# One product of the rational unit moved from VectorE to GpSimd in sixteen units, with its constant added by ScalarE

## The chip, the core and the metric

The kernel runs on one core of a Trainium2 chip. The metric is the device time of one execution in microseconds (us), the median of several. Engines are TensorE (PE in the rows; PEld is its weight load), VectorE (DVE), ScalarE (ACT), GpSimd (POOL) and SyncE (SP), which issues DMAs.

## What is computed

Three stages follow each other: a gated linear attention (4 batches, 8 heads, 768 steps, head width 48), a two-layer network with a rational activation (384 to 2048 to 384, 3072 tokens), and a second network with a softmax-like activation and a layer norm (384 to 1024 to 384). The change touches the rational activation:

```python
h = x @ w_in
h2 = h * h
h3 = h2 * h
P = a[0] + a[1] * h + a[2] * h2 + a[3] * h3
Q = 1.0 + np.abs(b[0]) * np.abs(h) + np.abs(b[1]) * h2
g = P / (Q + 1e-06)
return (g @ w_out).astype(np.float32)
```

## The kernel before

The tokens are cut into 6 chunks of 512. For every chunk the hidden layer of 2048 is cut into 16 blocks of 128. One chunk with one block is a **unit**; there are 96, numbered u = 0 to 95, and the first 16 are the first chunk.

A unit has two halves. `m_up(u)` multiplies the block of `w_in` with the chunk (nine matmuls at L590: three slices of 128, each as high x high, high x low and low x high part), which leaves `hp`, 128 x 512, in PSUM; then it works out g in `p`; at the end ScalarE writes its high part `gh` (L623) and GpSimd the rest `gl` (L624). `m_down(u)` adds the unit's part to the three sums `x2p` (nine matmuls at L636) and is written four units later (LAG = 4).

With numerator and denominator brought to squares by constants, `p` starts as (h + beta1)^2 (L597) and `w` as (|h| + beta2)^2 (L598); Q up to a factor is then `w` plus a constant column, `rest`. ScalarE works out a first inverse as exp(-ln(w + rest)), and one Newton step makes it exact enough: inverse times (2 - Q times inverse). The product of Q and the first inverse is what the change is about. Two forms stand side by side:

- **even units below 24** (MIX): VectorE folds the numerator into `hp` (L608), ScalarE takes the logarithm (L609) and the exponential (L610) into `ah`, GpSimd adds `rest` to `w` (tensor_scalar, L611) and multiplies by `ah` (tensor_tensor, L612), VectorE multiplies numerator and inverse (L613) and finishes with L614. That makes three VectorE steps.
- **all others**: VectorE's L616, ScalarE's logarithm (L617) and exponential into `hp` (L618), then VectorE's L619 (the product, with the constant added), L620 and L621. That makes four VectorE steps.

Buffers: `hp` has three in PSUM, so unit u+3's first product waits for the last reader of unit u's. `ah`, `w`, `gh` and `gl` have two each, `p` three.

Beside the first 16 units two other strands run. Weights arrive in four groups of four blocks; `split_w` joins two words of a float64 into a float32 on VectorE (L535, L538, L539), takes the high part on ScalarE (L545) and the low part on GpSimd (L546). Groups 2 and 3 are split while units 0 to 8 run. And the attention of the following halves is prepared: transposes (L290, L295, L324) and scans (L308, L317) on VectorE, scores (L420), masks on GpSimd (L428), outputs (L444) and states (L483) on TensorE.

The order on each engine is not that of the source: a scheduler places every instruction from its own estimate of time, within dependences and buffers. Each engine then works through its order without overtaking.

Of the kernel before, what the change touches and what calls it, by code (L numbers as in the profile page):

```python
# [12 lines left out]
AF = mybir.ActivationFunctionType  # L13
ALU = mybir.AluOpType
# [16 lines left out]
def kernel(  # L31
# [15 lines left out]
    nc = tc.nc  # L47
# [9 lines left out]
    NF1 = DF1 // 128  # L57
# [21 lines left out]
    MIX = lambda u: u < 24 and u % 2 == 0  # L79
# [73 lines left out]
    def network(fast):  # L153
# [424 lines left out]
        fin = {}  # L578
# [4 lines left out]
        def m_up(u):  # L583
            c, f = divmod(u, NF1)
            n, o = divmod(f, 4)
            hp = ps_hp.tile([128, NTOK], F32, name="hp", tag="h")
            hi, lo = wi[n]
            for kt in range(KT):
                for w, xx in ((hi, 0), (hi, 1), (lo, 0)):
                    last["PE", u] = nc.tensor.matmul(  # L590
                        hp, lhsT=w[:, kt, 128 * o:128 * o + 128], rhs=xts[c][:, kt, xx, :],
                        start=(kt == 0 and w is hi and xx == 0), stop=(kt == KT - 1 and w is lo),
                    )
            ah, w, p = (moe_pool.tile([128, NTOK], F32, name=nm, tag=nm, bufs=NB[nm]) for nm in ("ah", "w", "p"))
            nc.scalar.activation(ah, hp, AF.Abs)  # L595
            if fast:
                nc.scalar.activation(p, hp, AF.Square, bias=co[:, 7:8])  # L597
                nc.scalar.activation(w, ah, AF.Square, bias=co[:, 6:7])  # L598
                rest = co[:, 8:9]
            else:  # L600
                nc.scalar.activation(p, hp, AF.Identity, bias=ab[:, 2:3], scale=ab[:, 3:4])
                nc.gpsimd.tensor_scalar(w, ah, babs[:, 1:2], babs[:, 0:1], ALU.mult, ALU.add)
                nc.gpsimd.tensor_tensor(w, w, ah, ALU.mult)
                nc.vector.tensor_tensor(p, p, hp, ALU.mult)
                rest = qc
            a1, a0 = (co[:, 9:10], a0s) if fast else (ab[:, 1:2], ab[:, 0:1])
            if fast and MIX(u):
                nc.vector.scalar_tensor_tensor(hp, p, a1, hp, ALU.add, ALU.mult)  # L608
                nc.scalar.activation(ah, w, AF.Ln, bias=rest)  # L609
                nc.scalar.activation(ah, ah, AF.Exp, scale=-1.0)  # L610
                nc.gpsimd.tensor_scalar(w, w, rest, 1.0, ALU.add, ALU.mult)  # L611
                nc.gpsimd.tensor_tensor(w, w, ah, ALU.mult)  # L612
                nc.vector.scalar_tensor_tensor(hp, hp, a0, ah, ALU.add, ALU.mult)  # L613
                fin[u] = nc.vector.scalar_tensor_tensor(p, w, 2.0, hp, ALU.subtract, ALU.mult, reverse0=True)  # L614
            else:
                nc.vector.scalar_tensor_tensor(p, p, a1, hp, ALU.add, ALU.mult)  # L616
                nc.scalar.activation(ah, w, AF.Ln, bias=rest)  # L617
                nc.scalar.activation(hp, ah, AF.Exp, scale=-1.0)  # L618
                nc.vector.scalar_tensor_tensor(w, w, rest, hp, ALU.add, ALU.mult)  # L619
                nc.vector.scalar_tensor_tensor(hp, w, 2.0, hp, ALU.subtract, ALU.mult, reverse0=True)  # L620
                fin[u] = nc.vector.scalar_tensor_tensor(p, p, a0, hp, ALU.add, ALU.mult)  # L621
            gh, gl = (moe_pool.tile([128, NTOK], F32R, name=nm, tag=nm, bufs=NB[nm]) for nm in ("gh", "gl"))
            last["ACT", u] = nc.scalar.activation(gh, p, AF.Copy)  # L623
            last["POOL", u] = nc.gpsimd.tensor_tensor(gl, p, gh[:].bitcast(F32), ALU.subtract)  # L624
            gts[u] = (gh, gl)
# [246 lines left out]
        for u in range(NU + LAG):  # L872
# [6 lines left out]
            if u < NU:  # L879
                if f == 0 and c == NCH - 1:  # L880
                    if fast:
                        judge(moe_pool)
                    open2()
                    tail = chain(w2_load("i"), n_load(0), w2_load("o"))
                if f == 0 and c and not fast:
                    x_load(c)
                if fast and u < NF1:
                    if f % 4 == 0:
                        _run(prep)
                        prep = w1_group(f // 4 + 2) if f < 8 else iter(())  # L890
                    with later(G1):
                        take(prep, 1)
                m_up(u)
                if fast and u < NF1:
                    with later(G1):
                        take(prep, 1)
# [157 lines left out]
```

## Time and profile before

| what | value |
|---|---|
| times of three runs | 785.37, 786.02, 788.82 us |
| median | 786.02 us |
| the profiled execution | 786.76 us |
| its span, first to last instruction | 784.9 us |
| mean granted TensorE clock | 0.962 |
| TensorE, busy | 730.2 us (93%) |
| VectorE, busy | 639.8 us (82%) |
| ScalarE, busy | 534.5 us (68%) |
| GpSimd, busy | 359.9 us (46%) |

A busy share over the whole span mixes stretches with different limits, so such a table only says where to look; what a step is worth is read in the stretch in which it runs. The granted clock is the share of TensorE's full speed (2.4 GHz) that the chip allowed.

### The profile page before, as it was taken

The page shows a single profiled execution, that of the slowest core. Times are in us where ns is not written, and L with a number is a line of the kernel's source. Part 1 is how long each engine was busy: PE and PEld are TensorE (multiplying, and loading weights), DVE is VectorE, ACT ScalarE, POOL GpSimd, SP SyncE. Part 2 cuts the span into 40 slices and gives each one's busy share as a digit, 9 for nine tenths or more (in the row PEclk, how much of TensorE's full clock was granted, in tenths as well). Part 3 has the DMA queues.
Part 4 walks back from the last instruction along what each step waited for, and adds up shares of the span by engine and source line. Part 5 has one row for each costly group of instructions (what it writes and reads, how often), then busy time and mean ns, then how long its engine had stood idle before and what let it go on. Part 6 is the DMA issues. An engine that isn't in the chain of part 4 may idle for free.

```text
span 784.9 us, 13904 instructions
## 1 busy us (share of the span) xinstructions
PE 730.2 (93%) x4976; PEld 605.3 (77%) x4976; DVE 639.8 (82%) x1110; ACT 534.5 (68%) x983; POOL 359.9 (46%) x306
## 2 busy tenths in 40 slices
PE   4775896999999999999999999999999999999996
PEld 3654674778887788777878788888888989988996
DVE  5999999989899998989898966567887688777640
ACT  2245656779886888788978888788865555555541
POOL 3256677766755344444554433243233433352322
PEclk9767699899999999999999999999999999999998
DMA  7865547373858175536736250640024353542552
GB/s 172 239 201 174 142 154 158 114 182 115 189 167 208 57 196 134 146 83 208 157 121 122 82 121 2 228 175 0 1 82 101 115 120 90 140 102 57 139 121 72
DMA packets 87278, 101.74 MB, mean 130 GB/s; under 512 B 34464, under 2 KB 63136, under 8 KB 87200
## 3 DMA queue, kind: packets, MB, share of 16 engines
q1 hardware_dynamic: 87104, 100.67, 48.5%
q8 instruction: 41, 0.67, 0.4%
q14 instruction: 37, 0.30, 0.1%
q10 hardware_dynamic: 96, 0.10, 0.0%
HBM read 60.59 MB, written 27.56 MB: 112 GB/s over the span
## 4 chain that ended last, share of the span: by engine, by line
DVE 28%; PE 17%; ACT 13%; issue 5%; SPq 4%; DMA 4%; POOL 1%; ACTq 0%; DVEq 0%; POOLq 0%
PE x2p L636 6%; PE hp L590 6%; DVE room L750 3%; SPq L760 3%; DVE room L733 2%; PE op L774 2%; ACT jk L735 2%; DVE p L616 2%; DVE hp L620 2%; DVE w L619 2%; DVE sm L729 2%; DMA room<-room 2%; DMA rq<-in_q_dram 2%; DVE room L748 2%; PE h L710 2%
## 5 line engine op out<-in xcount | busy, mean ns | idle before, releaser
L590 PE MATMUL hp<-xt,g 128*128 128x512 f32 x864 | 225.0, 402 | 9.5 <-DVE alT L302 4.0
L624 POOL TENSOR_TENSOR gl<-p,gh 128x512 fp32r<-128x512 f32 x96 | 127.9, 1332 | 190.2 <-ACT gh L623 104.1
L590 PEld LDWEIGHTS hp<-xt,g 128*128 128x128 f32 x864 | 163.2, 192 | 50.0 <-DVE p L621 5.0
L636 PE MATMUL x2p<-gh,g 128*128 128x512 f32 x576 | 197.5, 397 | 2.8 <-ACT x2e L644 2.1
L636 PEld LDWEIGHTS x2p<-gh,g 128*128 128x128 f32 x576 | 108.6, 189 | 30.5 <-ACT x2e L644 4.7
L636 PE MATMUL x2p<-gl,g 128*128 128x512 f32 x288 | 113.6, 394 | 1.8 <-POOL gl L624 1.8
L774 PE MATMUL op<-w2oh,room 128*128 128x384 f32 x384 | 101.8, 339 | 1.2 <-DVE room L766 0.6
L766 POOL TENSOR_TENSOR room<-room,room 128x1024 fp32r<-128x1024 f32 x22 | 54.6, 2484 | 101.1 <-ACT room L765 79.7
L619 DVE SCALAR_TENSOR_TENSOR w<-w,co,hp 128x512 f32<-128x512 f32 x84 | 62.0, 738 | 44.2 <-ACT hp L618 43.3
L710 PE MATMUL h<-w2ih,x 128*128 128x512 f32 x288 | 90.7, 394 | 0.0
L597 ACT ACTIVATE p<-hp,co 128x512 f32<-128x512 f32 x96 | 65.9, 687 | 13.0 <-POOL gl L624 12.8
L618 ACT ACTIVATE hp<-ah 128x512 f32<-128x512 f32 x84 | 50.1, 596 | 32.8 <-DVE p L616 31.6
L774 PEld LDWEIGHTS op<-w2oh,room 128*128 128x128 f32 x384 | 70.1, 188 | 2.8 <-DVE room L766 1.0
L616 DVE SCALAR_TENSOR_TENSOR p<-p,co,hp 128x512 f32<-128x512 f32 x84 | 61.8, 736 | 10.2 <-ACT p L597 9.9
L598 ACT ACTIVATE w<-ah,co 128x512 f32<-128x512 f32 x96 | 69.4, 724 | 0.7 <-DVE hp L620 0.3
L595 ACT ACTIVATE ah<-hp 128x512 f32<-128x512 f32 x96 | 56.5, 589 | 13.7 <-PE hp L590 13.6
L636 PEld LDWEIGHTS x2p<-gl,g 128*128 128x128 f32 x288 | 54.2, 188 | 15.0 <-POOL gl L624 3.1
L623 ACT ACTIVATE gh<-p 128x512 fp32r<-128x512 f32 x96 | 59.9, 624 | 7.8 <-PE x2p L636 2.7
L774 PE MATMUL op<-w2ol,room 128*128 128x384 f32 x192 | 65.0, 339 | 0.0
L710 PEld LDWEIGHTS h<-w2ih,x 128*128 128x128 f32 x288 | 53.9, 188 | 11.7
L621 DVE SCALAR_TENSOR_TENSOR p<-p,co,hp 128x512 f32<-128x512 f32 x84 | 61.9, 737 | 1.1
L617 ACT ACTIVATE ah<-w,co 128x512 f32<-128x512 f32 x84 | 60.5, 721 | 1.2
(168 smaller groups left out, 1274.8 us busy)
## 6 DMA issues: line engine op xcount, KB each, us to landing
room<-room SPq DMA_DIRECT2D x96, 128.0 KB, 2.4
qk_d<-qk SPq DMA_DIRECT2D x10, 771.0 KB, 4.4
st<-in_moe_w_in_dram SPq DMA_DIRECT2D x15, 512.0 KB, 4.6
st<-in_moe_w_out_dram SPq DMA_DIRECT2D x18, 384.0 KB, 3.5
qks<-qk_d SPq DMA_DIRECT2D x20, 257.0 KB, 5.2
x<-x_d SPq DMA_DIRECT2D x18, 256.0 KB, 3.4
out_dram<-o SPq DMA_DIRECT2D x94, 48.0 KB, 1.6
ra<-in_alpha_dram SPq DMA_DIRECT2D x44, 96.0 KB, 2.3
```

The lines of the kernel that those rows point to most:

```text
L590: last["PE", u] = nc.tensor.matmul(hp, lhsT=w[:, kt, 128 * o:128 * o + 128], rhs=xts[c][:, kt, xx, :], start=(kt == 0 and w is hi and xx = ...
L597: nc.scalar.activation(p, hp, AF.Square, bias=co[:, 7:8])
L598: nc.scalar.activation(w, ah, AF.Square, bias=co[:, 6:7])
L616: nc.vector.scalar_tensor_tensor(p, p, a1, hp, ALU.add, ALU.mult)
L617: nc.scalar.activation(ah, w, AF.Ln, bias=rest)
L619: nc.vector.scalar_tensor_tensor(w, w, rest, hp, ALU.add, ALU.mult)
L621: fin[u] = nc.vector.scalar_tensor_tensor(p, p, a0, hp, ALU.add, ALU.mult)
L623: last["ACT", u] = nc.scalar.activation(gh, p, AF.Copy)
L624: last["POOL", u] = nc.gpsimd.tensor_tensor(gl, p, gh[:].bitcast(F32), ALU.subtract)
L636: nc.tensor.matmul(x2ps[c][d], lhsT=w[:, o, 128 * d:128 * d + 128], rhs=gg, start=(f == 0 and w is hi and gg is gh), stop=(f == NF1 - 1 an ...
L710: nc.tensor.matmul(hp[:, 512 * n:512 * n + 512], lhsT=x2s[c][:, kt, x, CH * b:CH * b + CH], rhs=w2[w][:, kt, 512 * n:512 * n + 512], start ...
L774: nc.tensor.matmul(op, lhsT=x[:, 128 * f:128 * f + 128], rhs=w2[w][:, f, :], start=(f == 0 and x is hi and w == "oh"), stop=(f == NF2 - 1 ...
```

## The change

For u below NF1 = 16 every unit, odd or even, takes three VectorE steps and GpSimd's product. The constant that GpSimd added in the even units is now added by ScalarE, as an Identity activation with `rest` as its bias, between the logarithm and the exponential. Units 16 to 23 keep the form of before by parity, and the others their own.

```diff
             a1, a0 = (co[:, 9:10], a0s) if fast else (ab[:, 1:2], ab[:, 0:1])
-            if fast and MIX(u):
+            if fast and u < NF1:
+                nc.vector.scalar_tensor_tensor(hp, p, a1, hp, ALU.add, ALU.mult)
+                nc.scalar.activation(ah, w, AF.Ln, bias=rest)
+                nc.scalar.activation(w, w, AF.Identity, bias=rest)
+                nc.scalar.activation(ah, ah, AF.Exp, scale=-1.0)
+                nc.gpsimd.tensor_tensor(w, w, ah, ALU.mult)
+                nc.vector.scalar_tensor_tensor(hp, hp, a0, ah, ALU.add, ALU.mult)
+                fin[u] = nc.vector.scalar_tensor_tensor(p, w, 2.0, hp, ALU.subtract, ALU.mult, reverse0=True)
+            elif fast and MIX(u):
                 nc.vector.scalar_tensor_tensor(hp, p, a1, hp, ALU.add, ALU.mult)
                 nc.scalar.activation(ah, w, AF.Ln, bias=rest)
                 nc.scalar.activation(ah, ah, AF.Exp, scale=-1.0)
```

Since the scheduler lays out all engines anew, other work moves too. In the changed program the lines of the units below 16 are L608 (numerator), L609 (logarithm), L610 (constant), L611 (exponential), L612 (product), L613 and L614; `gh` is L631, `gl` L632, and L636 becomes L644.

VectorE, before, at the end of unit 9, whose tiles are `p_1335`, `w_1334` and `hp_1323` (`hp_1358` is unit 10, `hp_1424` unit 11, `ft_1241` the last weight split, `P_1413` a scan of the attention):

```order
L538 SCALAR_TENSOR_TENSOR ft_1241<-st_1242,ft_1241 128x384
L308 SCALAR_TENSOR_TENSOR P_1413<-alT_111,d1_109 128x774
L619 SCALAR_TENSOR_TENSOR w_1334<-w_1334,co_85,hp_1323 128x512
L539 SCALAR_TENSOR_TENSOR ft_1241<-st_1242,ft_1241 128x384
L608 SCALAR_TENSOR_TENSOR hp_1358<-p_1370,co_85,hp_1358 128x512
L620 SCALAR_TENSOR_TENSOR hp_1323<-w_1334,hp_1323 128x512
L616 SCALAR_TENSOR_TENSOR p_1436<-p_1436,co_85,hp_1424 128x512
L621 SCALAR_TENSOR_TENSOR p_1335<-p_1335,co_85,hp_1323 128x512
```

VectorE, changed, at the same place (unit 9 is `p_1339`, `hp_1327`; unit 10 `hp_1363`; the last weight split `ft_1244`):

```order
L302 MEMSET alT_111 128x6x2
L608 SCALAR_TENSOR_TENSOR hp_1327<-p_1339,co_85,hp_1327 128x512
L539 SCALAR_TENSOR_TENSOR ft_1244<-st_1245,ft_1244 128x384
L290 STREAM_TRANSPOSE alT_111<-ra_1152 128x2x4x32
L608 SCALAR_TENSOR_TENSOR hp_1363<-p_1375,co_85,hp_1363 128x512
L290 STREAM_TRANSPOSE alT_111<-ra_1152 128x2x4x32
L295 STREAM_TRANSPOSE alT_111<-ra_1152 128x4x32
L613 SCALAR_TENSOR_TENSOR hp_1327<-hp_1327,co_85,ah_1337 128x512
L295 STREAM_TRANSPOSE alT_111<-ra_1152 128x4x32
L308 SCALAR_TENSOR_TENSOR P_1418<-alT_111,d1_109 128x774
L614 SCALAR_TENSOR_TENSOR p_1339<-w_1338,hp_1327 128x512
```

Unit 9's last step now follows the scan at once, and the last weight split stands ahead of the transposes instead of behind the scan.

TensorE, before, around the first product of unit 11 (`hp_1424`; `sc` are scores, `gh_1271` and `gl_1272` belong to unit 7):

```order
L420 MATMUL sc_1385<-qks_112 128x128
L420 MATMUL sc_1386<-qks_112 128x128
L590 MATMUL hp_1424<-xt_356,g2_751 128x512 x9
L636 MATMUL x2p0_1091<-gh_1271,g1_629 128x512
L636 MATMUL x2p0_1091<-gl_1272,g1_629 128x512
```

TensorE, changed, at the same place (unit 11 is `hp_1429`; `gh_1197` and `gl_1198` belong to unit 6, `gh_1275` to unit 7):

```order
L420 MATMUL sc_1390<-qks_112 128x128
L420 MATMUL sc_1391<-qks_112 128x128
L644 MATMUL x2p0_1093<-gl_1198,g1_629 128x512
L644 MATMUL x2p0_1093<-gh_1197,g1_629 128x512
L644 MATMUL x2p1_1094<-gl_1198,g1_629 128x512
L644 MATMUL x2p1_1094<-gh_1197,g1_629 128x512
L644 MATMUL x2p2_1095<-gl_1198,g1_629 128x512
L644 MATMUL x2p2_1095<-gh_1197,g1_629 128x512
L644 MATMUL x2p0_1093<-gh_1275,g1_629 128x512
L644 MATMUL x2p1_1094<-gh_1275,g1_629 128x512
L644 MATMUL x2p2_1095<-gh_1275,g1_629 128x512
L590 MATMUL hp_1429<-xt_356,g2_751 128x512 x9
```

Nine matmuls of the second product, which all stood elsewhere, now stand between the scores and unit 11.

## Rows read from the trace of the kernel before

**Rows 1.** By stretch (us): length, PE, PEld, DVE, ACT, POOL busy, clock, DMA:

```profile
71.00:147.20 76.20, 58.29 (x370) 44.30 (x370) 74.23 (x111) 48.99 (x90) 52.93 (x44) 0.84 0.62 165
147.20:209.00 61.80, 60.45 (x529) 48.63 (x530) 56.88 (x95) 51.73 (x94) 44.23 (x40) 1.00 0.52 146
```

**Rows 2.** TensorE's timeline: start, us, operation, count, [idle before <- releaser]:

```profile
131.57 1.16 PE L420 MATMUL sc<-qks 48*128 48x128 f32 x16
...
136.75 4.21 PE L590 MATMUL hp<-xt,g 128*128 128x512 f32 x9 [4.02 <-DVE alT L302]
...
147.22 2.32 PE L590 MATMUL hp<-xt,g 128*128 128x512 f32 x9 [0.24 <-DVE p L621]
```

**Rows 3.** Chain that ended last: start, us, what; nine matmuls at full clock:

```profile
457.90 2.04 PE x2p L636 x9
```

**Rows 4.** VectorE's groups, 71 to 147 us: busy, mean ns, idle before:

```profile
L539 DVE SCALAR_TENSOR_TENSOR ft<-st,ft 128x384 int32<-128x384 int32 x8 | 7.5, 934 | 0.0
L538 DVE SCALAR_TENSOR_TENSOR ft<-st,ft 128x384 int32<-128x384 int32 x8 | 6.4, 797 | 0.0
L539 DVE SCALAR_TENSOR_TENSOR ft<-st,ft 128x512 int32<-128x512 int32 x6 | 6.2, 1028 | 0.1
L535 DVE TENSOR_SCALAR ft<-st 128x384 int32<-128x384 int32 x8 | 6.2, 769 | 0.7 <-DMA st<-in_moe_w_out_dram 0.7
L538 DVE SCALAR_TENSOR_TENSOR ft<-st,ft 128x512 int32<-128x512 int32 x5 | 5.9, 1195 | 0.0
L608 DVE SCALAR_TENSOR_TENSOR hp<-p,co,hp 128x512 f32<-128x512 f32 x6 | 4.5, 745 | 0.0
L616 DVE SCALAR_TENSOR_TENSOR p<-p,co,hp 128x512 f32<-128x512 f32 x6 | 4.4, 735 | 0.0
L308 DVE TENSOR_TENSOR_SCAN P<-alT,d 128x774 f32<-128x774 f32 x2 | 4.4, 2184 | 0.0
L613 DVE SCALAR_TENSOR_TENSOR hp<-hp,co,ah 128x512 f32<-128x512 f32 x5 | 3.8, 752 | 0.0
L619 DVE SCALAR_TENSOR_TENSOR w<-w,co,hp 128x512 f32<-128x512 f32 x5 | 3.6, 728 | 0.0
L621 DVE SCALAR_TENSOR_TENSOR p<-p,co,hp 128x512 f32<-128x512 f32 x5 | 3.6, 726 | 0.1
L620 DVE SCALAR_TENSOR_TENSOR hp<-w,hp 128x512 f32<-128x512 f32 x5 | 3.4, 685 | 0.1
L614 DVE SCALAR_TENSOR_TENSOR p<-w,hp 128x512 f32<-128x512 f32 x5 | 3.4, 672 | 0.0
L535 DVE TENSOR_SCALAR ft<-st 128x512 int32<-128x512 int32 x5 | 3.3, 661 | 1.0 <-POOL w L611 0.6 <-issue 0.4
```

**Rows 5.** VectorE's timeline, three instructions:

```profile
79.31 0.68 DVE L538 SCALAR_TENSOR_TENSOR ft<-st,ft 128x512 int32<-128x512 int32 x1
79.91 0.68 DVE L614 SCALAR_TENSOR_TENSOR p<-w,hp 128x512 f32<-128x512 f32 x1
...
139.64 0.54 DVE L539 SCALAR_TENSOR_TENSOR ft<-st,ft 128x384 int32<-128x384 int32 x1
```

**Rows 6.** GpSimd's groups, 71 to 147 us, the two of the even units:

```profile
L612 POOL TENSOR_TENSOR w<-w,ah 128x512 f32<-128x512 f32 x5 | 8.9, 1773 | 0.2
L611 POOL TENSOR_SCALAR w<-w,co 128x512 f32<-128x512 f32 x6 | 5.3, 878 | 2.3 <-ACT ah L609 2.2
```

**Rows 7.** GpSimd's timeline, two instructions with the idle time before them:

```profile
81.33 1.27 POOL L624 TENSOR_TENSOR gl<-p,gh 128x512 fp32r<-128x512 f32 x1 [2.88 <-ACT gh L623]
...
140.47 2.72 POOL L428 TENSOR_SCALAR_AFFINE_SELECT A<-A 128x512 f32<-128x512 f32 x2 [1.69 <-ACT A L427]
```

**Rows 8.** ScalarE's groups, 71 to 174 us:

```profile
L609 ACT ACTIVATE ah<-w,co 128x512 f32<-128x512 f32 x8 | 5.8, 722 | 0.1
L610 ACT ACTIVATE ah<-ah 128x512 f32<-128x512 f32 x8 | 5.0, 629 | 0.1
L618 ACT ACTIVATE hp<-ah 128x512 f32<-128x512 f32 x8 | 4.7, 592 | 3.0 <-DVE p L616 3.0
```

## Prediction before the run

> **What bounds the kernel now.** I read three views in this order: the busy time of each engine by stretch, the matrix engine's timeline around its largest wait, and the groups of instructions by form inside the stretch that the change touches.
>
> The first 16 units run from about 71 to 174 us. Up to 147.2 us VectorE is busy for 74.23 of 76.2 us, while TensorE stands at a mean granted clock of 0.84, ScalarE at 48.99 and GpSimd at 52.93 us [rows 1]. That is a VectorE stage: it does its share of the units, splits the weights of two groups and prepares an attention half. From 147.2 us TensorE takes over: up to 209 us, where unit 24 begins, it is busy for 60.45 of 61.8 us, at full clock [rows 1]. So a gain is to be had only before about 147 us; afterwards TensorE must do its work whatever the others do.
>
> The joint is visible in TensorE's rows. The first product of unit 11 starts at 136.75 us after 4.02 us of idle time, and its nine matmuls take 4.21 us, twice the 2.04 us of nine at full clock: the clock had fallen to its lower level (1.2 of 2.4 GHz) in the wait [rows 2, 3]. Only three `hp` buffers exist, so unit 11 waits for the last VectorE step of unit 8 (the trace names the memset that stands behind it, L302). Unit 12 starts at 147.22 us, released by the last step of unit 9, L621 [rows 2].
>
> **What the change removes.** Odd units lose one VectorE step. Their four (L616, L619, L620, L621) have means of 735, 728, 685 and 726 ns, together 2.87 us; the three that stay (L608, L613, L614) have 745, 752 and 672 ns, 2.17 us [rows 4]. The saving is 0.70 us of busy time. Neighbours overlap a little: L538 starts at 79.31 and lasts 0.68, L614 follows at 79.91 [rows 5], so 0.08 us of each is hidden, and a step taken out gives 0.70 - 0.08 = 0.62 us. Even units lose GpSimd's tensor_scalar, 0.878 us each [rows 6].
>
> **What it adds.** Sixteen ScalarE instructions (the constant). No row shows this function; its neighbours with 512 columns cost 0.63 us (L610, no bias) and 0.72 us (L609, with a bias column) [rows 8]. It reads a bias column, so I take 0.72: ten of them by the end of unit 9 are 7.2 us on an engine with 76.2 - 48.99 = 27.2 us of idle time in that stretch [rows 1]. I cost it at nothing on the path; its cover is the backlog of VectorE, and the third rival is what happens where that cover is thin. Odd units also bring GpSimd one product each, 1.773 us by L612 [rows 6]. Five by unit 9 are 8.9 us; five tensor_scalar less are 4.4 us; net 4.5 us on an engine with 23.3 us idle [rows 1].
>
> **What GpSimd's extra work does to VectorE.** The weight splits read two SBUF tiles. Alone, one with 512 columns took 0.68 us (at 79.31 us) and one with 384 columns 0.54 (at 139.64) [rows 5]; GpSimd sat idle then, for 2.88 us until 81.33 and for 1.69 us until 140.47 [rows 7]. Their means in the stretch are 1.195 and 1.028 us with 512 columns, 0.797 and 0.934 with 384 [rows 4]. The excess is 5 x 0.515 + 6 x 0.348 + 8 x 0.257 + 8 x 0.394 = 9.9 us beside 52.93 us of GpSimd work, 0.19 us per us. The unit steps, which have `hp` in PSUM, show 0.67 to 0.75 us throughout [rows 4]. If the removed tensor_scalar had cost VectorE as much per us as a product, the extra is 4.5 x 0.19 = 0.8 us; if it had cost nothing, 8.9 x 0.19 = 1.7 us. I take 0.8, because VectorE's L535 has a wait of 0.6 us on L611 in its row [rows 4], which speaks for collisions of the tensor_scalar too.
>
> The Trainium skill ("SBUF — State Buffer", section "Who interferes with whom") says that a VectorE instruction with two SBUF inputs contends with a GpSimd instruction that reads SBUF, that one with at most one SBUF input outside the two-port modes does not, and that the loser blocks fully. The rows agree with both halves. By that rule the tensor_scalar, a reader of SBUF, counts like a product, which is the 0.8 end; with the 1.7 end the forecast below would be 0.9 us later.
>
> **Where the scheduler puts things.** It moves every engine's work up to unit 23; from unit 24 on TensorE's order is the same in both. Up to the last step of unit 9 VectorE has 254 instructions before and 248 after, six unit steps fewer and nothing else (the excerpts in the section on the change show its end). Up to the last step of unit 8 it has 237 in both: five unit steps fewer, but five split steps pulled forward (two L535, two L538, one L539).
>
> **The sum.** Unit 9's end comes 6 x 0.62 = 3.7 us earlier, less 0.8: at 147.2 - 2.9 = 144.3 us. Unit 8's end comes later: two L535 at 0.769, two L538 at 0.797 and one L539 at 0.934 [rows 4] are 4.07 us, 3.7 after overlap; 5 x 0.62 = 3.1 goes off; with most of the extra collisions (0.6) it is 1.2 us later, so unit 11 starts at 138.0 instead of 136.75. But nine second-product matmuls now stand between the scores and unit 11, which shortens the idle time. Behind unit 11 TensorE needs 2.04 (its product) + 2.04 (nine) + 1.1 (scores, 1.16 in [rows 2]) = 5.2 us at full clock: unit 12 could start at 143.2, so unit 9 sets it, at 144.3, 2.9 us earlier than now. At the low level through the product and the first of the nine (4.0 + 2.4 + 1.1) it starts at 145.5, 1.7 us earlier. By then TensorE has done 75 second-product matmuls instead of 81; the six that it owes are 6 x 2.04 / 9 = 1.4 us, and by unit 15 both orders have done the same number. Net: 1.5 us gained at full clock, 0.3 at the low one. I take 1.5, because the idle time before unit 11 shrinks (about 2.0 us of the 4.02 are filled). From there TensorE is the bound in both, so the 1.5 us arrive at the end.
>
> The profiled execution took 786.76 us, with a span of 784.9, so 1.9 us lie around the span; the median of the three runs is 786.02, 0.7 below the profiled one. 784.9 - 1.5 = 783.4, plus 1.9 is 785.3; against the median, 786.0 - 1.5 = **784.5 us**.
>
> **Rivals.** Half a per cent, 3.9 us, is about what a measurement of this kernel can tell from no change: faster means below 782.1, slower above 789.9.
>
> *The full harvest.* The extra collisions don't come (the product replaces a tensor_scalar that collided longer), and half of VectorE's remaining idle time, 76.2 - 74.23 = 2.0 us, closes too, since ScalarE's exponential no longer waits for VectorE to release `hp` (the even units' exponential, L610, shows 0.1 us of waiting, the odd units' L618 3.0 [rows 8]). Then unit 9 ends at 147.2 - 3.7 - 1.0 = 142.5, unit 12 follows at once, and the 1.4 us owed fit into TensorE's idle time from 147.2 to 209 us (61.8 - 60.45 = 1.35 [rows 1]): 147.2 - 142.5 = 4.7 us, **781.3 us**. Against it: unit 8 does not come earlier in the new order, and TensorE needs its 5.2 us behind it.
>
> *Collisions eat it.* With 1.7 us of extra collisions and the low clock in unit 11, unit 8 ends 0.7 us later still, unit 12 starts at 146.2, 1.0 earlier, and 1.4 are owed: 0.4 us lost, **786.4 us**. For it: the low clock is there now. It is no change to a measurement.
>
> *A loop through two buffers, slower.* `ah` and `w` have two buffers each. In odd units `ah` was free after the exponential and `w` after L620; now both stay until the last steps, as in even units. Unit u+2's square (L598) therefore waits for unit u's L614, and ScalarE, which works in order, stops with it. The loop is the square, at L609's 0.72, + L609 0.72 + constant 0.72 + L610 0.63 [rows 8] + product 1.77 [rows 6] + L614 0.67 [rows 4] = 5.2 us for two units, in which TensorE needs at least 4 x 2.04 = 8.2. It decides once more than 3.0 us of other work stand in front of its members. The place is units 10 to 15, behind the score masks: two take 2.72 us of GpSimd (at 140.47 us), a `gl` 1.27 (at 81.33 us) [rows 7], and VectorE's scan L308 2.18 [rows 4], together 6.2, 3.2 too many, in the two pairs that have masks: 6.4 lost, 1.5 gained, **790.9 us**. Against it: L614 shows no wait for GpSimd's product in this stretch (0.0 [rows 4]), and in the new order other VectorE work stands between L613 and L614 in each of the units 0 to 9.
>
> That the change doesn't do what it says I leave out: the order shows 16 products and 16 constants.
>
> **How the numbers follow.** The forecast gets 0.46, the full harvest 0.25, collisions 0.18, the loop 0.11. Faster takes most of the harvest, of which some stays above 782.1, and the early tail of the forecast: 0.24. Slower is the loop: 0.11. Same is the rest: 0.65. The range reaches a little past the harvest's 781.3, to 780.6, and over the collisions' 786.4 by as much as an unpriced reordering of the units 0 to 8 may cost (the 1.2 us of unit 8), to 787.8; the loop and the far tails stay out.
>
> **What would show it.** Right: nine matmuls of unit 11 at about 2 us and less idle time before them; unit 12 at about 144 us; VectorE still above 95% up to there; TensorE's wait for GpSimd's `gl` no longer than now; the same distance from unit 24 to the end. Wrong: VectorE waiting for L612 by more than 3 us in all (the loop); unit 12 at 147 or later with L538 and L539 above their present means (collisions); or a changed distance from unit 24 to the end, which my sum takes as fixed.

## The result and the profile after

The change makes the kernel slower by 0.9%: the changed kernel's median is 792.32 us (12 runs, 789.90 to 798.04) beside 785.86 us of the kernel before, timed beside it (12 runs), a ratio of 1.0091 with a 95% interval of 1.0070 to 1.0112. The forecast was 784.5 us. Of all the runs in this document one, the slowest of e9 (799.94 us), was in the chip's slower state, and it is left out of e9's ratio. The profiled execution took 793.3 us; its page begins so (share of the span, number of instructions):

```profile
span 791.6 us, 13929 instructions
...
PE 731.5 (92%) x4976; PEld 609.7 (77%) x4976; DVE 635.8 (80%) x1102; ACT 544.4 (69%) x999; POOL 362.5 (46%) x306
```

The same two stretches as in [rows 1], by the same columns:

```profile
71.00:147.20 76.20, 53.11 (x340) 42.36 (x341) 69.28 (x100) 51.03 (x93) 50.40 (x41) 0.82 0.59 158
147.20:209.00 61.80, 58.28 (x498) 46.76 (x496) 54.70 (x86) 53.03 (x98) 46.98 (x41) 0.97 0.54 153
```

In the stretch where VectorE was the bound, VectorE is now idle for 76.2 - 69.28 = 6.9 us instead of 2.0, and TensorE does 5.2 us less. This stretch is cut by the clock, so it can't tell whether VectorE had less to do for the same units. A cut from 71 us, up to which VectorE has worked through 146 instructions in either kernel, to the end of a unit can. To unit 8's end before and after, and to unit 9's end after (before is the first of [rows 1]):

```profile
71.00:136.70 65.70, 48.07 (x327) 36.62 (x327) 63.77 (x93) 40.42 (x74) 45.89 (x38) 0.86 0.63 166
71.00:143.70 72.70, 49.61 (x325) 39.45 (x326) 65.78 (x94) 47.53 (x87) 47.87 (x38) 0.81 0.60 161
71.00:150.70 79.70, 56.61 (x364) 45.23 (x364) 72.75 (x104) 53.16 (x97) 53.90 (x43) 0.83 0.59 157
```

Up to unit 8's end VectorE is busy for 2.0 us more, and its idle time grows from 1.9 to 6.9 us: together unit 8 is 7.0 us late. Up to unit 9's end it is busy for 74.23 - 72.75 = 1.5 us less, and its idle time grows by 5.0 us too: unit 9 is 3.5 us late. So what comes on top of VectorE's work is waiting.

The ends of the units (the last VectorE step of each, us, from the timelines of the profiled executions; the columns on the right belong to experiments below) show where the time is lost:

```
unit   before  after   e9     e10    e12    e15
0       80.6    80.7   80.5   82.0   80.6   81.2
4      109.3   113.9  110.5  114.4  111.5  111.7
5      117.5   124.1  118.6  124.2  116.1  120.2
8      136.7   143.7  138.6  144.3  140.9  135.5
9      147.2   150.7  151.8  151.3  145.5  144.9
12     160.1   167.0  164.4  167.2  163.0  161.1
15     176.5   182.5  182.9  181.8  178.4  175.8
24     220.3   226.7  225.9  226.2  220.8  219.1
28     241.8   247.9  248.3  247.5  241.8  239.7
```

Unit 28 is 6.1 us late. At unit 4 it is already 4.6 us and at unit 8 7.0, but at unit 9 only 3.5, and at unit 12 6.9 again, so the distance is not built up step by step. From unit 28 to unit 90 it stays at 6.1 to 6.2 us, and the spans differ by 6.7.

TensorE's timeline of after (start, us, operation, count, idle time and releaser), to set beside [rows 2]:

```profile
103.30 0.75 PE L444 MATMUL y<-A,vns 128*32 128x128 f32 x17 [3.16 <-POOL A L428]
...
106.83 4.75 PE L590 MATMUL hp<-xt,g 128*128 128x512 f32 x18
...
132.85 4.21 PE L590 MATMUL hp<-xt,g 128*128 128x512 f32 x9 [5.66 <-DVE p L614]
...
145.04 2.20 PE L590 MATMUL hp<-xt,g 128*128 128x512 f32 x9
...
150.85 2.35 PE L590 MATMUL hp<-xt,g 128*128 128x512 f32 x9
```

The wait that stood before unit 11 (4.02 us, then nine matmuls at the lower clock level) has not gone; it stands before unit 9 now, 5.66 us long, and is paid with the same 4.21 us for nine matmuls. (The rows at 145.04 and 150.85 are the first products of units 11 and 12.) A new wait of 3.16 us stands at 103.30 inside the attention's `y` matmuls, and the first products of units 5 and 6 (18 matmuls in one row) queue behind it.

GpSimd's timeline shows what that wait was for:

```profile
96.64 0.64 POOL L428 TENSOR_SCALAR_AFFINE_SELECT A<-A 128x512 f32<-128x512 f32 x1 [2.75 <-ACT A L427]
97.86 2.80 POOL L612 TENSOR_TENSOR w<-w,ah 128x512 f32<-128x512 f32 x1 [0.58 <-ACT ah L611]
100.62 1.31 POOL L546 TENSOR_TENSOR g<-ft,g 128x384 fp32r<-128x384 f32 x1
101.89 1.35 POOL L428 TENSOR_SCALAR_AFFINE_SELECT A<-A 128x512 f32<-128x512 f32 x1
```

Unit 3's new product, 2.80 us long, and a split's last step stand between the two score masks (L428).

VectorE's waits in the same stretch, 71 to 147 us (waiting line, releaser: us in all, times, longest):

```profile
DVE ft L535 <- DMA st<-in_moe_w_in_dram: 3.4, 2, 1.7
DVE ft L535 <- POOL A L428: 2.0, 1, 2.0
DVE hp L613 <- ACT ah L611: 1.1, 1, 1.1
```

Before, L535 waited 0.7 us for a transfer and 1.0 for others [rows 4]. One of the two waits for a transfer (1.66 us, at 77.82) lies before unit 0's end, where the two kernels are still level. And two of ScalarE's waits of after in that stretch, before it writes the buffer `ah`:

```profile
ACT ah L595 <- DVE hp L613: 2.0, 1, 2.0
...
ACT ah L595 <- POOL w L612: 1.8, 1, 1.8
```

### The profile page after: what moved, and what is told of

The parts are those of the page before. It is cut to its first block, busy times and chain, and to the rows that moved or that the text cites. A ratio compares the mean times of both kernels' runs of the same rounds, so it can differ in the third digit from the quotient of the medians.

```text
span 791.6 us, 13929 instructions
## 1 busy us (share of the span) xinstructions
PE 731.5 (92%) x4976; PEld 609.7 (77%) x4976; DVE 635.8 (80%) x1102; ACT 544.4 (69%) x999; POOL 362.5 (46%) x306
## 4 chain that ended last, share of the span: by engine, by line
PE 44%; DVE 25%; ACT 10%; DMA 8%; issue 7%; SPq 3%; POOL 3%; DVEq 0%; ACTq 0%; POOLq 0%
PE h L718 13%; PE op L782 12%; PE x2p L644 9%; PE hp L590 8%; DMA st<-in_moe_w_in_dram 2%; SPq L266 2%; DVE p L624 2%; DVE hp L628 2%; DVE alT L324 2%; DVE w L627 2%; DVE qk L290 2%; DVE ft L539 2%; DVE ft L538 1%; DMA st<-in_moe_w_out_dram 1%; ACT hp L626 1%
## 5 line engine op out<-in xcount | busy, mean ns | idle before, releaser
L632 POOL TENSOR_TENSOR gl<-p,gh 128x512 fp32r<-128x512 f32 x96 | 128.0, 1334 | 195.5 <-ACT gh L631 113.7
L644 PE MATMUL x2p<-gh,g 128*128 128x512 f32 x576 | 194.9, 394 | 1.4 <-ACT x2e L652 1.4
L644 PEld LDWEIGHTS x2p<-gh,g 128*128 128x128 f32 x576 | 108.5, 189 | 27.3 <-ACT x2e L652 3.3
L644 PE MATMUL x2p<-gl,g 128*128 128x512 f32 x288 | 113.6, 394 | 1.2 <-POOL gl L632 1.2
L627 DVE SCALAR_TENSOR_TENSOR w<-w,co,hp 128x512 f32<-128x512 f32 x76 | 56.0, 737 | 43.1 <-ACT hp L626 42.3
L595 ACT ACTIVATE ah<-hp 128x512 f32<-128x512 f32 x96 | 56.6, 590 | 23.1 <-PE hp L590 14.9
L626 ACT ACTIVATE hp<-ah 128x512 f32<-128x512 f32 x76 | 45.4, 598 | 29.2 <-DVE p L624 28.3
L644 PEld LDWEIGHTS x2p<-gl,g 128*128 128x128 f32 x288 | 54.5, 189 | 13.8 <-POOL gl L632 1.6
L631 ACT ACTIVATE gh<-p 128x512 fp32r<-128x512 f32 x96 | 60.0, 625 | 6.8 <-PE x2p L644 3.3
L624 DVE SCALAR_TENSOR_TENSOR p<-p,co,hp 128x512 f32<-128x512 f32 x76 | 55.9, 736 | 10.2 <-ACT p L597 10.0
L718 PE MATMUL h<-w2il,x 128*128 128x512 f32 x144 | 57.3, 398 | 0.0
L629 DVE SCALAR_TENSOR_TENSOR p<-p,co,hp 128x512 f32<-128x512 f32 x76 | 56.1, 738 | 1.0
```

The costliest lines, as they stand in the source:

```text
L644: nc.tensor.matmul(x2ps[c][d], lhsT=w[:, o, 128 * d:128 * d + 128], rhs=gg, start=(f == 0 and w is hi and gg is gh), stop=(f == NF1 - 1 an ...
L718: nc.tensor.matmul(hp[:, 512 * n:512 * n + 512], lhsT=x2s[c][:, kt, x, CH * b:CH * b + CH], rhs=w2[w][:, kt, 512 * n:512 * n + 512], start ...
```

## The experiments

A note on reading them: the kernels were timed in rounds beside the kernel before, and the profile is one execution of each. Five theories are used. A: the products on GpSimd cost the time. B: the constants on ScalarE do. C: the order into which the scheduler puts all engines does. C2 is C after e9 and e10; V and P ask for the engine. In kernels with an order table the line numbers are shifted (111 lines in e9, 113 in e12 and e16; e12's L727 is L614).

**Parts of the change.** Each of the first four changes the condition of the new form only (the line of e1; the others have `u % 2 == 1`, `u < 9` and `8 < u < NF1`).

```diff
-            if fast and u < NF1:
+            if fast and u < NF1 and u % 2 == 0:
```

> Only the even units below 16 take the new form: their constant goes from GpSimd to ScalarE, the odd units stay as before. Theory A (the loss of 6.5 us comes from the odd units' product on GpSimd, which stands in front of masks and gl): no change to before, 785 to 787 us. Theory B (it comes from the 16 constants on ScalarE, whose order holds up everything behind them): half of the loss, 788 to 790 us. Theory C (it comes from the new order of all engines, whatever the added work is): anything, with the weight splits pulled ahead of unit ends.

> Only the odd units below 16 take the new form; the even units keep GpSimd's tensor_scalar for the constant. Theory A: the whole loss or more, 792 to 795 us, since GpSimd keeps its tensor_scalar beside the products. Theory B: half of the loss, 788 to 790 us.

> Only units 0 to 8 take the new form; up to unit 8 VectorE's order is that of the changed kernel. If the loss is made in the VectorE stage (PE's unit 9 starts 8 us later in the trace, 5 us of which remain by unit 15): 790 to 792 us. If it is made by the longer chain beside a saturated TensorE, in units 9 to 15: 785 to 787 us.

> Only units 9 to 15 take the new form; up to unit 8 the order is that of before. If the loss is made in the VectorE stage: 785 to 787 us, since four odd units save VectorE steps where TensorE is the bound. If it is made in units 9 to 15: 789 to 792 us, with TensorE waiting for unit ends between 150 and 210 us.

Measured: e1 783.28 us, ratio 0.9979 (0.9961 to 0.9998); e2 784.0, 0.9978 (0.9967 to 0.9990); e3 789.84, 1.0054 (1.0034 to 1.0075); e4 783.48, 0.9967 (0.9944 to 0.9990). Either half of the units, even or odd, gains about 0.2%, together they lose 0.9%. Neither A's nor B's range holds for e1 or e2. e2 already has all 16 products on GpSimd, so A falls as a simple price per product; e1 moves eight constants to ScalarE and gains, so B falls as a simple price per constant. The new form in the units 0 to 8 alone is enough for a loss, of 0.5% (just under the range of 790 to 792 us), and in the units 9 to 15 alone it gains 0.3%. Both together lose 0.9% and not 0.2, so the parts don't add up: every variant also has an order of its own.

**Single edges in the queues.** If the order is to blame, perhaps one displaced piece is. e5 takes after and puts VectorE's weight splits back between the unit ends where before has them; e6 takes before and displaces them as in after; e7 takes after and puts unit 3's product behind the second mask. The edges order a queue and wait for nothing (`first` and `third` are a split's first and third VectorE step; HOLD and KEEP name split and unit, in e6 KEEP alone; MASKED is e7's):

```diff
+        def behind(x, ins):
+            tc.add_manual_dep(
+                x.ins, ins.ins.name, mybir.DependencyInfo(mybir.DependencyClass.NoSync, mybir.DependencyReason.DATA),
+                reason="queued behind",
+            )
...
+    HOLD = ((16, 1, 0), (17, 1, 1), (18, 2, 2), (20, 4, 4), (22, 5, 5), (23, 6, 6), (24, 7, 7), (26, 8, 8))
...
+                    for x, at, fu in HOLD:
+                        if u == at:
+                            behind(first[x], fin[fu])
+                    for x, at, fu in KEEP:
+                        if u == at:
+                            behind(fin[fu], third[x])
...
+    MASKED = ((3, (2, 1, 1), 3),)
...
+            for at, m, n in MASKED:
+                if fast and u == at:
+                    behind(prod[n], mask[m])
```

> The kernel after with the same instructions; only VectorE's order is changed: queue-order edges put the weight-split steps 17 to 28 at the places between the unit ends that they have before (22, 23, 24 and 26 splits ahead of the ends of units 5, 6, 7 and 8, where the kernel after has 23, 25, 26 and 27). Theory C (the scheduler's new order loses the time, by splits pulled ahead of unit ends): the loss of 6.5 us goes; 783 to 786 us, and no end of units 4 to 8 more than 1 us later than before. Theory A+B (16 products on GpSimd and 16 constants on ScalarE cost it by themselves, whatever the order): 791 to 793 us.

> The kernel before with the same instructions; only VectorE's order is changed the other way: the ends of units 2 and 4 to 8 are queued behind the splits that stand ahead of them in the kernel after (23, 25, 26 and 27 splits ahead of the ends of units 5 to 8). Theory C: slower than before, by 3 to 6 us (789 to 792), with ends of units 5 to 8 that come 3 us or more later. Theory A+B: within 1 us of before, 785 to 787 us.

> The kernel after with one queue-order edge: GpSimd's product of unit 3 is queued behind the second score mask of the half step beside it, so that TensorE's y matmuls do not wait 3.2 us for the mask and unit 5's first product, which stands behind them, starts earlier than 106.8 us. If that one wait is the loss: 6 us come back, 785 to 787 us. If the loss is spread over VectorE's order (theory C): 1 to 3 us come back, 789 to 791 us, and the wait of 5.7 us before unit 9's second product stays. Theory A+B: 791 to 793.

Measured: e5 791.48 us, 1.0057 (1.0034 to 1.0080); e6 790.85, 1.0055 (1.0030 to 1.0080); e7 790.13, 1.0043 (1.0022 to 1.0064). e6 agrees with C: the same instructions, with the splits displaced, lose 0.55%. e5 does not: with the splits back in place most of the loss stays. e7 gives back 2.2 us of after's median, as C said of it (by the ratios, 1.0043 beside 1.0091, it is nearer to 4), and the wait for the mask shrinks from 3.16 to 2.00 us. TensorE's longest wait for a unit's end does not stay at 5.7 us, as C had it; it is 3.5 there. e5 gives back 0.8 us by the medians and 2.7 by the ratios, whose intervals overlap. The traces of e5 and e6 can't be used for the loss: the profiled executions took 786.62 and 787.17 us and were the fastest and the second of ten (e5 ranges to 794.48, e6 to 793.40), with unit 28 within 0.6 us of its time in before. In e6's, the ends of units 5 to 7 come 2.6 to 5.7 us later than before and unit 8's comes on time, so a late unit end in between need not be a loss.

**The constant on GpSimd.** e8 is the kernel before with the even units' form (product and constant on GpSimd) in all 16:

```diff
-    MIX = lambda u: u < 24 and u % 2 == 0
+    MIX = lambda u: u < 16 or (u < 24 and u % 2 == 0)
```

> All 16 products on GpSimd as after, but the constant added by GpSimd too, as the even units have it before: no unit instruction is added to ScalarE, and GpSimd gets 16 instructions of about 0.88 us. Theory B (the 16 constants on ScalarE, behind whose queue splits and masks wait): faster than after by 3 us or more, 786 to 789 us. Theory C: its order has as many splits ahead of unit ends 4 to 8 as after (21, 23, 24, 26, 27), so about as slow, 789 to 793 us.

Measured: 790.19 us, 1.0041 (1.0019 to 1.0063), within the range of C. A loss of 0.4%, about half of after's 0.9, is there with no new instruction on ScalarE; the order is once more its own.

**Work and order taken apart.** The decisive runs hold the order of all five queues fixed. A table names each queue's instructions of the units 0 to 35, and each is queued behind the one ahead of it:

```diff
+            if fast and u == 36:
+                in_order()
...
+        def in_order():
+            at = {i.name: i for i in nc.cur_bb.bb.instructions}
+            for row in ORDER:
+                for a, b in zip(row, row[1:]):
+                    tc.add_manual_dep(
+                        at[f"I-{b}"], f"I-{a}",
+                        mybir.DependencyInfo(mybir.DependencyClass.NoSync, mybir.DependencyReason.DATA), reason="given order",
+                    )
```

> The kernel after with the same instructions; queue-order edges put every engine's instructions of the units 0 to 35 (1740 in five queues) in the order that they have before. Only the eight new products of the odd units on GpSimd are left to the scheduler, and each new constant on ScalarE stands right behind its unit's Ln. Theory C (the loss is made by the order into which the scheduler put the work around the moved instructions, on all engines together): the loss of 6.5 us goes, and VectorE's missing eight instructions show: 782 to 785.5 us. Theory A+B (16 products on GpSimd and 16 constants on ScalarE cost it by themselves, through collisions and queues): 790 to 793 us.

> The kernel before with the same instructions, with every engine's instructions of the units 0 to 35 in the order that they have in the kernel after; the odd units' denominator step on VectorE and the even units' constant on GpSimd, which the kernel after does not have, are left to the scheduler. Theory C: as slow as after or slower, since VectorE has eight instructions more in the same order: 791 to 796 us. Theory A+B: 784 to 787 us, as before.

e11 keeps after's order and drops one line:

```diff
-                nc.scalar.activation(w, w, AF.Identity, bias=rest)
```

> The kernel after with the 16 additions of the constant on ScalarE left out (so the denominator of the first 16 units lacks its constant in that product), with every engine's other instructions held in the order of after. Prices the constants alone. Theory B: 3 us or more come back, 786 to 789 us. Theory C: 791 to 793 us, no more than 1.5 us faster than after.

Measured: e9 791.92 us (11 runs), 1.0076 (1.0048 to 1.0105); e10 792.39, 1.0084 (1.0053 to 1.0116); e11 789.28, 1.0059 (1.0029 to 1.0089). e10 is what C expects: the old instructions, in the new order, lose what the change loses. e9 is what A+B expects: the new instructions lose as much in the old order. So neither alone explains it. e11, with the 16 constants left out, is 3.0 us below after's median. But the ratios, 1.0059 and 1.0091, differ by 0.32%, with an error of about 0.37% worked out from their intervals, so that the constants cost time there is not shown.

e9's trace shows one reason why the new form does badly in the old order. Its ScalarE rows (149.22 is unit 11's absolute value, L595 in after):

```profile
144.39 0.71 ACT L709 ACTIVATE w<-ah,co 128x512 f32<-128x512 f32 x1
149.22 0.60 ACT L706 ACTIVATE ah<-hp 128x512 f32<-128x512 f32 x1 [4.12 <-DVE hp L724]
```

and the VectorE rows around it:

```profile
144.75 2.57 DVE L419 TENSOR_TENSOR_SCAN P<-alT,d 128x774 f32<-128x774 f32 x1
147.25 0.52 DVE L650 SCALAR_TENSOR_TENSOR ft<-st,ft 128x384 int32<-128x384 int32 x1
147.70 0.74 DVE L719 SCALAR_TENSOR_TENSOR hp<-p,co,hp 128x512 f32<-128x512 f32 x1
148.36 0.74 DVE L724 SCALAR_TENSOR_TENSOR hp<-hp,co,ah 128x512 f32<-128x512 f32 x1
150.43 0.75 DVE L719 SCALAR_TENSOR_TENSOR hp<-p,co,hp 128x512 f32<-128x512 f32 x1 [1.32 <-ACT p L708]
```

`ah` has two buffers. In the old odd form the exponential writes `hp`, and ScalarE itself frees `ah`. In the new form VectorE's L724 (L613 in after) frees it, and that step stands behind the scan. Unit 11's absolute value waits 4.12 us; unit 11's first VectorE step (150.43) waits for ScalarE in turn, and unit 9's last step stands behind it. Unit 9 ends 4.6 us later than before, and TensorE waits 3.79 us for that before unit 12. This is not all of e9's loss: 1.9 of the 4.6 us are there at unit 8's end.

The next three test C2, one with an order that the scheduler made for the odd half, two with after's:

> The kernel after with the same instructions, with every engine's instructions of the units 0 to 35 in the order of the kernel that has the new form in the odd units alone (784.0 us, all 16 products on GpSimd). The one difference to that kernel: the even units' constant is ScalarE's. Theory C2 (the order decides: after's work is not slow in an order that suits it; before's does not): 782 to 786 us. Theory A+B (16 products on GpSimd with 16 constants on ScalarE cost 6 us in whatever order): 789 to 793 us.

> The kernel with the new form in the odd units alone (784.0 us), with every engine's instructions of the units 0 to 35 in the order of after; the even units' constant on GpSimd, which after does not have, is left to the scheduler. Theory C2: after's order costs about 6 us whatever the work (the kernel before took 792.4 in it): 789 to 793 us. Theory A+B: 783 to 786 us.

> The kernel with the new form in the even units alone (783.3 us), with every engine's instructions of the units 0 to 35 in the order of after; the odd units' denominator step on VectorE, which after does not have, is left to the scheduler. Theory C2: 789 to 793 us. Theory A+B: 782 to 785 us.

Measured: e12 784.14 us, 0.9976 (0.9964 to 0.9989); e13 790.82, 1.0061 (1.0042 to 1.0079); e14 789.33, 1.0054 (1.0030 to 1.0077). All three as C2 expects. Set out by work (rows) and order (columns), medians in us, from several rounds (the kernel before had medians of 785.6 to 786.2 us in them):

```
                    its own   before's   odd half's   after's
before              786.0        -           -         792.4
new form, odd       784.0        -           -         790.8
new form, even      783.3        -           -         789.3
after               792.3      791.9       784.1         -
```

This settles it: after and e12 run the same instructions, one order takes 792.3 us and the other 784.1, with ratios whose intervals lie far apart. And the order of after costs 6.0 to 6.8 us with each of three other works.

How the two orders differ is seen from unit 0's end to unit 9's, in which both traces start at the same time (80.7 and 80.6 us); the columns are those of [rows 1]. After:

```profile
80.70:150.70 70.00, 56.61 (x364) 45.23 (x364) 64.79 (x93) 46.99 (x86) 48.69 (x39) 0.86 0.55 147
```

and e12:

```profile
80.60:145.50 64.90, 57.42 (x364) 43.65 (x364) 61.20 (x89) 47.52 (x85) 48.71 (x38) 0.88 0.56 146
```

TensorE has the same 364 matmuls. VectorE has 89 instructions ahead of unit 9's end instead of 93, which is 3.6 us less busy time, and 3.7 us of idle time instead of 5.2. So the larger part of the 5.1 us is other VectorE work that stands ahead of the unit's end, and the smaller is waiting. The two are furthest apart at unit 5's end, by 8.0 us. VectorE's rows of after around it (114.42 is unit 5's first step, 123.43 its last):

```profile
114.42 0.74 DVE L608 SCALAR_TENSOR_TENSOR hp<-p,co,hp 128x512 f32<-128x512 f32 x1
116.86 1.13 DVE L535 TENSOR_SCALAR ft<-st 128x512 int32<-128x512 int32 x1 [1.70 <-DMA st<-in_moe_w_in_dram]
118.02 1.66 DVE L538 SCALAR_TENSOR_TENSOR ft<-st,ft 128x512 int32<-128x512 int32 x1
119.60 0.74 DVE L608 SCALAR_TENSOR_TENSOR hp<-p,co,hp 128x512 f32<-128x512 f32 x1
120.26 1.09 DVE L539 SCALAR_TENSOR_TENSOR ft<-st,ft 128x512 int32<-128x512 int32 x1
121.28 0.75 DVE L613 SCALAR_TENSOR_TENSOR hp<-hp,co,ah 128x512 f32<-128x512 f32 x1
...
123.43 0.69 DVE L614 SCALAR_TENSOR_TENSOR p<-w,hp 128x512 f32<-128x512 f32 x1
```

and of e12 (first step at 110.16, last at 115.42):

```profile
110.16 0.72 DVE L721 SCALAR_TENSOR_TENSOR hp<-p,co,hp 128x512 f32<-128x512 f32 x1
...
112.65 0.74 DVE L726 SCALAR_TENSOR_TENSOR hp<-hp,co,ah 128x512 f32<-128x512 f32 x1
113.31 1.58 DVE L651 SCALAR_TENSOR_TENSOR ft<-st,ft 128x512 int32<-128x512 int32 x1
...
115.42 0.67 DVE L727 SCALAR_TENSOR_TENSOR p<-w,hp 128x512 f32<-128x512 f32 x1
```

In after a whole split, with a wait of 1.70 us for its weights' transfer, stands inside unit 5, whose last two steps queue behind it. In e12 no step inside unit 5 waits for a transfer, and its last step starts 5.3 us after its first instead of 9.0.

This is no full account. In e12 a whole split stands inside unit 6 instead, and by unit 8 the distance has shrunk to 2.8 us. Nor do waits for weights tell the two orders apart; e12's VectorE waits of the stretch from 71 to 147 us are

```profile
DVE ft L648 <- DMA st<-in_moe_w_out_dram: 2.8, 2, 2.2
DVE ft L648 <- DMA st<-in_moe_w_in_dram: 1.5, 2, 1.2
```

4.3 us, more than after's 3.4. The profiled execution of e12 was also the slowest of its 11 runs, 785.65 us, and its unit 28 ends when before's does.

**Which queue.** The last three put one engine's queue of the one order into the other. They are made like e9, with the table put together from two orders.

> The instructions of after in the odd units' order (784.1 us as a whole), but VectorE's queue alone in the order of after: 23, 25 and 26 weight splits ahead of the ends of units 5, 6 and 7 instead of 21, 23 and 25. Theory V (VectorE's order is the place of the loss): 788 to 792 us, with the end of unit 5 near 124 us. Theory P (TensorE's order is: unit 5's first product behind the y matmuls, which wait for GpSimd's mask): 783 to 786 us.

> The instructions of after in the odd units' order, but TensorE's queue alone in the order of after: all y matmuls of the half step, with their wait for the mask, ahead of unit 5's and unit 6's first products. Theory P: 788 to 792 us. Theory V: 783 to 786 us.

> The instructions of after in its own order (792.3 us), but TensorE's queue alone in the order of the odd units' kernel, so that unit 5's first product stands in the middle of the y matmuls. Theory P: 784 to 787 us. Theory V: 789 to 793 us, since the end of unit 5 still stands behind 23 splits on VectorE.

Measured: e16 806.55 us, 1.0246 (1.0211 to 1.0280); e17 796.23, 1.0137 (1.0104 to 1.0170); e18 796.33, 1.0126 (1.0076 to 1.0175). All three are slower than V or P expected. e16 and e17 are slower than either whole order; e18 is slower than the odd half's, and its interval overlaps with after's. In e16 TensorE waits for unit ends eight times (waits, 71 to 215 us):

```profile
PE hp L703 <- DVE p L727: 14.6, 8, 3.7
```

against 3.8 us in three times in e12. So neither VectorE's nor TensorE's queue alone holds the loss: either one is good only with the others that were laid out with it. Of the two, VectorE's was the dearer to exchange (22 us in the odd half's order, beside 12). The queues of ScalarE, GpSimd and SyncE were not exchanged alone. Which of after's misplacements costs how much stays open: undoing the mask's (e7) gave back 2 to 4 us, and undoing the splits' (e5) nothing that is clear of noise.

**A better kernel.** e15 has the new form in the even units below 9 and in all units from 9 to 15:

```diff
-            if fast and u < NF1:
+            if fast and u < NF1 and (u % 2 == 0 or u > 8):
```

> The new form in the even units below 9 and in all units from 9 to 15, ordered by the scheduler as it likes. Up to unit 8 VectorE's order between the unit ends is that of the kernel with even units alone. If its gain (2.3 us) and that of the late units (2.1 us) add up: 781 to 783 us. If a changed work needs its own order and the scheduler does not find it: 785 us or more.

Measured: 782.66 us, 0.9962 (0.9948 to 0.9975), the fastest of all and within the expected range for gains that add up (0.38%, beside 0.21 and 0.33). It is picked from several variants, so its lead over e1 and e4 (0.6 and 0.8 us) is no finding; its lead over before is. Its row for the first stretch of [rows 1]:

```profile
71.00:147.20 76.20, 58.76 (x380) 46.08 (x381) 71.82 (x113) 53.15 (x98) 49.21 (x41) 0.87 0.62 167
```

TensorE has done 380 matmuls by 147.2 us, before 370, after 340.

## Why the prediction was wrong, step by step

**The bound.** Right as a reading of before: VectorE set the pace up to 147.2 us, TensorE afterwards. What did not follow is that fewer steps for VectorE mean an earlier end. VectorE "still above 95%" was the sign asked for; it was 69.28 / 76.2 = 91%.

**The step that failed: where the scheduler puts things.** The text priced the new order by counting VectorE's steps ahead of the ends of units 8 and 9: unit 8's end 1.2 us later, unit 9's at 144.3 us, 2.9 earlier. Measured: unit 8 at 143.7, 7.0 later, and unit 9 at 150.7, 3.5 later. The cuts to the ends of units 8 and 9 show the term that failed: VectorE's waits, which the sum had put at nothing, and which grew by 5.0 us up to either end. A step whose input is late holds the queue: 1.66 us for a transfer at 77.82 us, 2.01 behind GpSimd's mask at 85.14, 1.70 for a transfer at 116.86, 1.13 for ScalarE at 139.93. The busy time was nearer to the sum: 2.0 us more up to unit 8 instead of 1.2, and 1.5 less up to unit 9 instead of 2.9. On TensorE the mask behind a product added a wait of 3.16 us. Which of these waits carries how much of the loss at the end is open; e12 has waits like the first two and is not slow. I had taken the reordering of the units 0 to 8 for something that widens the range by 1.4 us. The order is about the whole result, as e10 and e12 show.

**The work itself.** In another order the same instructions come to the forecast time: e12, 784.14 us, beside 784.5. That is an agreement of the number only. The sum was made for after's order, and e12 does not follow its steps: unit 12's first product starts at 145.60 us and not at 144.3, and unit 28 ends when it did before. Where e12 gains its 0.2% is not shown.

**Collisions, mis-sized.** The forecast took 0.8 us, at most 1.7. The splits of after, the same groups as in [rows 4]:

```profile
L538 DVE SCALAR_TENSOR_TENSOR ft<-st,ft 128x384 int32<-128x384 int32 x8 | 10.1, 1259 | 0.1
...
L539 DVE SCALAR_TENSOR_TENSOR ft<-st,ft 128x384 int32<-128x384 int32 x8 | 7.0, 878 | 0.1
...
L614 DVE SCALAR_TENSOR_TENSOR p<-w,hp 128x512 f32<-128x512 f32 x9 | 6.1, 674 | 0.0
L538 DVE SCALAR_TENSOR_TENSOR ft<-st,ft 128x512 int32<-128x512 int32 x5 | 5.9, 1184 | 0.0
L539 DVE SCALAR_TENSOR_TENSOR ft<-st,ft 128x512 int32<-128x512 int32 x6 | 5.7, 951 | 0.1
```

By the same reckoning the excess is 5 x 0.504 + 6 x 0.271 + 8 x 0.719 + 8 x 0.338 = 12.6 us, before 9.9: 2.7 more, though GpSimd is busy for 50.40 us instead of 52.93 in the stretch. So GpSimd's time alone does not set it. L538 with 384 columns went from 0.797 to 1.259 us, while the three other groups became a little shorter; in e12 it is 1.030 with the same products. That it depends on which step meets which is the likely reason; no run isolates it. The sign "L538 and L539 above their present means" thus came true for one group of four. The Trainium skill ("SBUF — State Buffer", section "Who interferes with whom") names who collides, and the rows agree again: the splits with two SBUF inputs are stretched, L614 with `hp` in PSUM is not. A price per microsecond of GpSimd's work, as I made it, does not hold in these rows.

**The constants at nothing.** One constant took 0.717 us in after (the mean of L610 from 71 to 174 us), as assumed. Whether they cost time on the path in after's order stays open: leaving them out (e11) gave 3.0 us by the medians, not clear of noise, and the old form takes 792.39 us in that order without any of them (e10). In the odd half's order eight more of them, with eight fewer constants on GpSimd, cost nothing that shows (e12 784.14, e2 784.0).

**The joint at unit 11.** The sign asked for came true, and the reading behind it was wrong: unit 11's nine matmuls took 2.20 us with no idle time before them, but they started at 145.04 us and not at 138.0. The idle time moved to unit 9, with the low clock level. Unit 12's first product started at 150.85 us, not 144.

**From unit 24 to the end.** The assumption held: 6.4 us late at unit 24, 6.7 in the span.

**The rivals.** The loop through two buffers came nearest in time (790.9 us, chance 0.11) and had a mechanism that exists: ScalarE is held before it writes `ah`, by VectorE's L613 (4.12 us at unit 11 in e9, 2.0 in after) or by GpSimd's product (1.8 in after). It was looked for in the wrong place, as VectorE waiting for L612 behind the masks in the units 10 to 15; that wait has no row up to 147 us, and its rows of units 11, 14 and 15 come to 1.6 us, under the 3 asked for. It also is not the main cause in after, since e10 loses as much with the old odd form. The chance of slower was too low because every case took the new order as nearly harmless.

## What to carry to other kernels

Where a scheduler lays out in-order queues, an edit of a few instructions deals all queues anew, and the new deal can cost more than the edit is worth: before pricing the instructions, look on each engine for what has moved ahead of steps that others wait for, steps with late inputs above all. To tell work from order, run the new instructions in an old order and the old ones in the new order, and then in a third, since both may lose. Try such a change in parts too: here either half gained 0.2%, a mixture 0.4%, and the whole lost 0.9%.

## What the runs showed that was not expected

How far the times of one kernel spread differs from order to order. e12 and e15 lie within 3.0 and 2.1 us over 11 and 8 runs; e9 lies between 787.99 and 797.74 over ten, e5 between 786.62 and 794.48. A slow order need not spread, though: e8 lies within 2.4 us over ten runs. Where it does, one profiled execution can miss the loss altogether, as in e5.

Exchanging one queue between two legal orders of the same instructions changed the time by 12 to 22 us (e17 and e16 against e12), about two to three and a half times what the change itself did (6.5 us).
